# Query pair products from shifted copies on VectorE, in place of selection matmuls and squares on ScalarE

## The chip, the cores and the metric

The kernel runs on one core of one Trainium2 chip. The metric is the device time of one execution in microseconds (us). A profiled execution also has a *span*, from the first to the last instruction; it is about 2 us shorter than the time of the same run. A run is slow here when it took over 1.5% longer than the fastest of the same kernel. Medians and ranges are those of all runs.

A ratio below is the mean time of one kernel's fast runs over the mean of the other's fast runs of the same rounds, with a 95% interval. It is therefore not quite the ratio of the medians that stand beside it.

## The reference, cut to what matters

Two independent attention problems, A and B, have the same shapes: 2048 tokens, width 640, 32 heads of 20. Inputs are bf16.

```python
def _A_ref(x, wqkv, wo):                       # softmax attention
    ...
    scores = jnp.einsum("bhqd,bhkd->bhqk", q, k) * (Dh ** -0.5)
    p = _softmax(scores, axis=-1)
    o = jnp.einsum("bhqk,bhkd->bhqd", p, v)
    return o.transpose(0, 2, 1, 3).reshape(B, S, D) @ wo
def _B_ref(x, wqkv, wo):                       # linear attention
    phi = lambda t: jnp.where(t > 0, t + 1, jnp.exp(t)) + 1e-6
    pq, pk = phi(q), phi(k)
    kv = jnp.einsum("bhsd,bhse->bhde", pk, v);  z = jnp.einsum("bhsd->bhd", pk)
    num = jnp.einsum("bhqd,bhde->bhqe", pq, kv)
    den = jnp.einsum("bhqd,bhd->bhq", pq, z)[..., None] + 1e-6
    o = num / den
    return o.transpose(0, 2, 1, 3).reshape(B, S, D) @ wo
return jnp.concatenate([a, b], axis=-1)
```

Both kernels avoid A's 2048 x 2048 scores. They replace the exponential by a polynomial of second degree. The keys enter through moments (sums over keys of 1, of k, and of products of two components of k, each with the value row), and each query then needs only its own 20 components and its 210 pair products.

## The kernel before

The work has three stages: A's key moments, A's query blocks, and the outputs. B's work is filler. A planner written in Python places every instruction beforehand, so each engine runs a fixed list in order and waits on semaphores. `PB, BK = 3.0, 1.02` are ranks in that planner; a lower number goes first.

A's queries are loaded four heads at a time. Selection matmuls of contraction 32, one for each head, form q_a + q_(a+d) for 110 and then for 100 of the 210 pairs of a head, and ScalarE squares them out of PSUM:

```python
    def t_sel(self, n, k, deps):
        ...
            for i in range(4):
                b = t.bank[i // 2] + i % 2
                sch.mm(ps[0:nb, b, :], self.S2[32 * i:32 * i + 32, 110 * k:110 * k + nb],
                       self.Qr[32 * i:32 * i + 32, s, g, :], start=True, stop=True, ...)
        ...
            def sq(x, p=p):
                b = j.bank[p]
                sch.op("act", lambda e: e.activation(self.psi[0:nb, sp, k, 2 * p:2 * p + 2, :], ps[0:nb, b:b + 2, :],
                                                     AF.Square, scale=sc), ...)
```

The moments are multiplied with q (four matmuls) and with the squares (eight), and VectorE evicts the 20 numerators and the denominator:

```python
    def t_pv(self, n, deps):
        ...
            for i in range(4):
                sch.mm(ps[32 * i:32 * i + 32, b, :], self.Mst[:, g, 32 * i:32 * i + 32], self.Qr[:, s, g, :], ...)
            for k in range(2):
                for i in range(4):
                    sch.mm(ps[32 * i:32 * i + 32, b, :], self.Tu[0:_NB[k], k, g, 32 * i:32 * i + 32],
                           self.psi[0:_NB[k], sp, k, i, :], start=False, stop=(k == 1), ...)
        ...
        def ev(_):
            sch.op("dve", lambda e: e.tensor_scalar(self.OTr[:, pr, u, :], ps[:, j.bank, :], self.cst[:, g:g + 1], 0.0,
                                                    op0=ALU.add, op1=ALU.max, accum_out=self.mx[:, n:n + 1]), ...)
```

Normalisation sends denominators to DRAM, takes reciprocals, reads them back broadcast, multiplies, stores to DRAM (`f_Od`) and reloads the result for the output projection. B's reciprocals also return by broadcast loads, 52 DMAs on SyncE's queue in all.

## Time and profile before

| what | before |
|---|---|
| time, median (range) | 398.18 us (397.9 to 400.53), 3 runs |
| span of the profiled run | 394.6 us |
| TensorE, VectorE, ScalarE busy | 315.4, 251.6, 232.9 us |
| mean granted TensorE clock | 0.905 of full |
| bytes moved by DMA | 42.48 MB |

The first fence is the top of the page of the kernel before. Each digit is the busy share of one fortieth of the span, in tenths; PEclk is the granted clock in tenths.

```profile
span 394.6 us, 14071 instructions
## 1 busy us (share of the span) xinstructions
PE 315.4 (80%) x6356; PEld 179.0 (45%) x6356; DVE 251.6 (64%) x444; ACT 232.9 (59%) x373; POOL 14.2 (4%) x43
## 2 busy tenths in 40 slices
PE   4278997999999899598879787787896896357485
PEld 1256766877676577432222233232342443235142
DVE  5859985876846988966625264575664877354431
ACT  1147864564757687448999975769785895010001
POOL 7600000000000000000000000000000000000000
PEclk9999999999999999779966867989898999587789
```

TensorE is near full in the first stage. In the middle ScalarE comes to 9 while VectorE falls and the clock drops. At the end nobody is full. The same by stage (a row is a stretch of time; busy us of each engine, then clock, DMA share and GB/s):

```profile
core 0: us, PE busy (x) PEld busy (x) DVE busy (x) ACT busy (x) POOL busy (x), PEclk, DMA share, GB/s
22.00:141.00 119.00, 112.97 (x3276) 84.17 (x3280) 87.46 (x135) 77.06 (x172) 0.00 (x0) 1.00 0.37 83
141.00:300.00 159.00, 131.73 (x1872) 57.64 (x1864) 98.75 (x176) 123.09 (x160) 0.00 (x0) 0.85 0.29 86
300.00:390.00 90.00, 64.22 (x1194) 33.86 (x1186) 49.16 (x96) 29.06 (x36) 0.00 (x0) 0.85 0.44 142
```

The groups of instructions that the change removes (busy us, mean ns of one, then the idle time before them and what ended it):

```profile
L1457 ACT ACTIVATE f_big<-ps 100x1024 bf16<-100x1024 f32 (+1 forms) x128 | 120.8, 1043 | 16.5 <-PE ps L172 16.3
...
L172 PE MATMUL ps<-f_Qr,f_S 32*110 32x512 bf16 (+1 forms) x256 | 41.4, 472 | 7.5 <-ACT f_big L1457 7.4
...
L1488 DVE TENSOR_SCALAR_CACHE_REDUCE f_xT<-ps,f_c 128x512 f32<-128x512 f32 x32 | 23.6, 736 | 20.1 <-PE ps L172 19.9
```

ScalarE's 120.8 us of squares look like the middle stage's limit: it is the engine with the most work there. That is read from the profile. The selection matmuls that feed them are TensorE time with no attention in it.

### The profile page before, as it was taken

To read this page: it belongs to the slowest core of one execution; us is meant where nothing else is said; L and a number is where in the kernel's file an instruction comes from. 1 tells how busy PE (TensorE), PEld (TensorE's weight loads), DVE (VectorE), ACT (ScalarE), POOL (GpSimd) and SP (SyncE) were. 2 spreads that over 40 slices of the span, in tenths; PEclk is the share of its full clock that TensorE was granted. 3 is DMA by queue.
4 is the path that set the end of the run, shared out by engine and by line. 5 is a ranking of instruction groups with operands and counts; after the bars stand their busy time and mean duration, and the time that the engine had idled before them with its cause. 6 is when DMAs were issued, how large, how long until landed. Compare 5 with 4: busy or idle time off the path is not lost.

```text
span 394.6 us, 14071 instructions
## 1 busy us (share of the span) xinstructions
PE 315.4 (80%) x6356; PEld 179.0 (45%) x6356; DVE 251.6 (64%) x444; ACT 232.9 (59%) x373; POOL 14.2 (4%) x43
## 2 busy tenths in 40 slices
PE   4278997999999899598879787787896896357485
PEld 1256766877676577432222233232342443235142
DVE  5859985876846988966625264575664877354431
ACT  1147864564757687448999975769785895010001
POOL 7600000000000000000000000000000000000000
PEclk9999999999999999779966867989898999587789
DMA  8996580000415201000023434347344644365232
GB/s 291 267 184 90 96 231 30 5 3 5 109 44 156 68 18 43 28 2 8 10 63 107 127 115 130 136 125 173 136 142 127 188 151 130 120 181 184 91 120 71
DMA packets 48913, 42.48 MB, mean 108 GB/s; under 512 B 23024, under 2 KB 44368, under 8 KB 48848
## 3 DMA queue, kind: packets, MB, share of 16 engines
q1 hardware_dynamic: 47536, 39.90, 36.1%
q10 hardware_dynamic: 1312, 1.64, 1.1%
q8 instruction: 50, 0.82, 0.9%
q14 instruction: 15, 0.12, 0.1%
HBM read 26.26 MB, written 10.83 MB: 94 GB/s over the span
## 4 chain that ended last, share of the span: by engine, by line
PE 43%; DMA 24%; DVE 17%; ACT 7%; issue 3%; SPq 3%; POOL 2%; DVEq 0%; POOLq 0%; ACTq 0%
PE ps L172 43%; DMA f_Rbc<-f_Nd 11%; DMA out_dram<-f_st 5%; DVE f_big L1298 4%; DMA f_big<-f_Nd 3%; ACT f_big L1457 3%; DMA f_w<-f_Od 3%; DVE f_r L1620 2%; DMA f_Nd<-f_Rc 2%; ACT f_ex L1624 2%; DVE f_big L1303 2%; DVE f_CT L1182 2%; SPq L1552 1%; DVE f_st L1069 1%; DVE f_OTw L1543 1%
## 5 line engine op out<-in xcount | busy, mean ns | idle before, releaser
L1457 ACT ACTIVATE f_big<-ps 100x1024 bf16<-100x1024 f32 (+1 forms) x128 | 120.8, 1043 | 16.5 <-PE ps L172 16.3
L172 PE MATMUL ps<-f_w,f_xT 128*32 128x320 bf16 x1280 | 49.7, 307 | 3.7 <-DVE f_xT L1069 3.7
L1069 DVE CAST f_st<-ps 128x320 bf16<-128x320 f32 x57 | 27.3, 486 | 35.3 <-PE ps L172 27.4
L172 PE MATMUL ps<-f_Qr,f_S 32*110 32x512 bf16 (+1 forms) x256 | 41.4, 472 | 7.5 <-ACT f_big L1457 7.4
L172 PE MATMUL ps<-f_wB,f_xB 128*32 128x320 bf16 x1280 | 45.9, 299 | 1.0 <-ACT f_ex L1624 1.0
L172 PE MATMUL ps<-f_woB,f_pk 128*32 128x320 bf16 x640 | 31.9, 356 | 14.7 <-DVE f_pk L1807 7.3
L1620 DVE TENSOR_SCALAR f_r<-ps 128x320 f32<-128x320 f32 (+1 forms) x52 | 29.2, 565 | 19.5 <-PE ps L172 12.1
L172 PEld LDWEIGHTS ps<-f_w,f_xT 128*32 128x32 bf16 x1280 | 34.6, 99 | 14.5 <-DVE f_xT L1069 4.0
L172 PEld LDWEIGHTS ps<-f_wB,f_xB 128*32 128x32 bf16 x1280 | 34.0, 97 | 11.9 <-ACT f_ex L1624 1.6
L1624 ACT ACTIVATE f_ex<-ps 128x320 f32<-128x320 f32 (+1 forms) x52 | 25.3, 498 | 22.9 <-DVE f_r L1620 14.5
L172 PE MATMUL ps<-f_wo,f_w 128*32 128x320 bf16 (+1 forms) x584 | 28.7, 325 | 10.4 <-DMA f_w<-f_Od 8.9
L1488 DVE TENSOR_SCALAR_CACHE_REDUCE f_xT<-ps,f_c 128x512 f32<-128x512 f32 x32 | 23.6, 736 | 20.1 <-PE ps L172 19.9
L1065 ACT CAST f_st<-ps 128x320 bf16<-128x320 f32 x7 | 2.9, 427 | 56.3 <-PE ps L172 34.8
L172 PEld LDWEIGHTS ps<-f_woB,f_pk 128*32 128x32 bf16 x640 | 18.6, 113 | 27.5 <-DVE f_pk L1807 8.5
L172 PE MATMUL ps<-f_xB,f_wB 128*32 128x512 bf16 x400 | 29.5, 426 | 1.9 <-ACT f_ex L1624 1.8
L172 PEld LDWEIGHTS ps<-f_Qr,f_S 32*110 32x110 bf16 (+1 forms) x256 | 12.3, 127 | 41.1 <-ACT f_big L1457 20.6
L1298 DVE TENSOR_TENSOR f_big<-f_big,f_Ks 128x3200 bf16<-128x3200 bf16 x16 | 28.9, 1820 | 1.8 <-ACT f_Ks L1065 1.8
L172 PE MATMUL ps<-f_big,f_Tu 110*32 110x512 bf16 (+1 forms) x256 | 26.2, 441 | 1.1 <-ACT f_big L1457 0.9
L172 PEld LDWEIGHTS ps<-f_wo,f_w 128*32 128x32 bf16 (+1 forms) x584 | 16.3, 103 | 22.3 <-DMA f_w<-f_Od 10.0
L1065 ACT CAST f_big<-ps 128x320 bf16<-128x320 f32 x29 | 12.1, 427 | 23.6 <-PE ps L172 21.9
L172 PE MATMUL ps<-f_xT,f_w 128*32 128x512 bf16 x400 | 23.8, 379 | 1.1 <-ACT f_Vp L1065 1.1
L1303 DVE TENSOR_TENSOR f_big<-f_big 128x2560 bf16<-128x2560 bf16 x16 | 23.7, 1484 | 0.0
(114 smaller groups left out, 369.0 us busy)
## 6 DMA issues: line engine op xcount, KB each, us to landing
out_dram<-f_st SPq DMA_DIRECT2D x32, 160.0 KB
f_Rbc<-f_Nd SPq DMA_DIRECT2D x8, 512.0 KB
f_big<-f_Nd SPq DMA_DIRECT2D x7, 512.0 KB
f_w<-f_Bd SPq DMA_DIRECT2D x12, 240.0 KB
f_Qd<-f_qkp SPq DMA_DIRECT2D x20, 128.0 KB
f_Qr<-f_Qd SPq DMA_DIRECT2D x16, 160.0 KB
f_wB<-in_B_wqkv_dram SPq DMA_DIRECT2D x3, 800.0 KB
f_Od<-f_OTw SPq DMA_DIRECT2D x60, 40.0 KB
```

Source lines behind the costliest of these rows:

```text
L172: lambda e: e.matmul(out, lhsT, rhs, start=start, stop=stop, tile_position=tp, skip_group_check=sgc),
L1065: return self.sch.op("act", lambda e: e.copy(out, in_), reads=reads, writes=writes)
L1069: return self.sch.op("dve", lambda e: e.tensor_copy(out, in_), reads=reads, writes=writes)
L1182: sch.op("dve", lambda e: e.tensor_copy(self.CT0[:], self.ident[:, 0:110]), reads=("ident",), writes=("CT0",))
L1298: sch.op("dve", lambda e: e.tensor_tensor(F[:, :, 112:212].rearrange("p h (d a) -> p h d a", a=20), k0.unsqueeze(2).broadcast_to([128, 32, ...
L1303: sch.op("dve", lambda e: e.tensor_tensor(F[:, :, 22:102].rearrange("p h (d a) -> p h d a", a=20), k0.unsqueeze(2).broadcast_to([128, 32, ...
L1457: sch.op("act", lambda e: e.activation(self.psi[0:nb, sp, k, 2 * p:2 * p + 2, :], ps[0:nb, b:b + 2, :], AF.Square, scale=sc), reads=(("ps" ...
L1488: sch.op("dve", lambda e: e.tensor_scalar(self.OTr[:, pr, u, :], ps[:, j.bank, :], self.cst[:, g:g + 1], 0.0, op0=ALU.add, op1=ALU.max, ac ...
L1543: sch.op("dve", lambda e: e.tensor_tensor(self.OTw[:, ow], self.OTr[:, pr], self.Rbc[rb], op=ALU.mult), reads=(("Rbc", rb, 0), ("Rbc", rb, ...
L1552: self.ost[P] = self.spd([lambda e, i=i: e.dma_start(dst(i), self.OTw[32 * i + 1:32 * i + 21, ow, :, :]) for i in range(4)], (m,), (("OTw" ...
L1620: sch.op("dve", lambda e: e.tensor_scalar(r1, ps[:, j.bank, 0:n], 0.0, 1e-6, op0=ALU.max, op1=ALU.add), reads=(("ps", j.bank),), writes=(( ...
L1624: sch.op("act", lambda e: e.activation(ex, ps[:, j.bank, 0:n], AF.Exp), reads=(("ps", j.bank),), writes=(("ex", k, h),))
```

## The change

Intent: six heads a block, so that 6 x 20 = 120 partitions are filled, and the pair products made as bf16 products on VectorE, q_a times q_(a+d), with the shift made by reading the queries from DRAM at another row. A full block loads six copies into a slot of 12 planes of 512 queries, VectorE makes ten planes of products out of them in three instructions (the last three over copies that are no longer wanted), ScalarE squares one plane, and TensorE multiplies all 12 with masked moments. There are 24 blocks (per 512 queries five of six heads, one of two heads) and three slots, so a slot is loaded again as soon as its block is multiplied.

```diff
-    NQR = 4
-    NPS = 3
+    NS = 3
+    NO = 9
+    NQK = 6
...
+    def t_psi(self, n, deps):
+        s = n % self.NS
+        sl = self.slot[0:120, s]
+        if c < 5:
+            fns = [lambda e: e.dma_start(sl[:, 0:4, :], self.q_load(c, qc, 0, 4, 1, True)),
+                   lambda e: e.dma_start(sl[:, 9:11, :], self.q_load(c, qc, 7, 2, 3, True))]
+        else:
...                                            # short block: six small loads
+            if c < 5:
+                mul(4, 9, 0, 4, (k0, k1, k2), (("sl", s, "A"),))     # 4 planes, 2048 elements
+                mul(8, 10, 0, 3, (k0, k1, k2), (("sl", s, "B"), k1)) # 3 planes
+                mul(1, 0, 1, 3, (k0, k2), (("sl", s, "C"), k2))      # 3 planes
...
     def t_pv(self, n, deps):
+            xs = (0, 1, 2, 3, 4, 5, 6, 7, 8, 9, 10, 11) if c < 5 else (1, 2, 3, 4)
+            for x in xs:
+                lhs = self.Tu[0:m, x, c, :] if c < 5 else self.TuS[0:m, x - 1, :]
+                self.fm(ps[0:126, b, :], lhs, self.slot[0:m, s, x, :], start=(x == xs[0]), stop=(x == xs[-1]), ...)
...                                            # normalisation in groups of three blocks,
...                                            # 25 small constants on GpSimd, masks for the moments
-        PB, BK = 3.0, 1.02
+        PB, BK = _C["bq"], _C["bk"]           # 4.77 and 2.57
```

The order changes too: A's keys now outrank B's keys and values, whose rank goes from 1.02 to 2.57. B's queries rank last of all, at 4.77.

## The prediction

> **What bounds it now (394.6 us profiled, 398.2 median).** Busy time by stretch shows three stages.
> - 22 to 164 us: key moments of A, with B's keys and values as filler. TensorE is busy 132.9 of 142 us at clock 1.00.
> - 172 to 335 us: A's queries. ScalarE is busy 130.7 of 163 us, 120.8 of it squares. TensorE shows 134.8, but in short bursts: by the waits it waits 33 us for squares; the granted clock is 0.87. Selection matmuls (41.4 us by group) stream only about 14 us of columns.
> - 335 to 395 us: the last outputs. TensorE works 34.7 of 60 us; the chain of waits runs through a 12.9 us broadcast, a 7.3 us reload, an 8.5 us store.
>
> **Removed.** ScalarE: 126 us of squares. TensorE: selection 41.4, linear term 15.5, moment matmuls 32.7: 90 us as the profile counts. VectorE: evictions with a maximum 26, normalisation 26, a 6.5 us start-up copy beside a 7 us GpSimd memset.
>
> **Added.** VectorE products: 2048+1536+1536 elements for 20 blocks, 2048 for four. Like products now do 3200 elements in 1.82 us, 2560 in 1.48, so 3.0 us and 1.3 us: 65 us. The Trainium skill ("VectorE: DVE Perf Modes", "What auto-detection actually checks") says an all-16-bit two-source product takes the two-results mode; 1.75 elements per ns agrees. Normalisation in threes 21 us, masks on the moments 12, guard 3. VectorE goes from 252 to an estimated 270, some copies moving to ScalarE, which falls from 233 to about 155.
> TensorE: 256 passes of 512 columns at the 0.24 us of today's dense query projection (23.8 us/100): 61 us, plus guard 7, building moments 5 to 8, projection 2. TensorE lands near 300 against 315, but denser.
> DMA: about 17 MB of shifted query loads and 2.6 MB of stores, minus 5: 42 to about 57 MB; DMA share in the query stage from 0.38 to perhaps 0.6; loads take 5 to 8 us, which three slots should cover.
>
> **Critical path.** A's moments now outrank B's keys and values, so they end after about 22 + 16 x 4.5 (VectorE features per tile) = 100 to 115 us instead of 164, plus some 12 us for masked moments. B's dense projections then fill TensorE beside the query blocks. The squares' bottleneck and most bubbles of 172 to 335 go; B's queries and reciprocals are made early, so part of the tail's 25 us of idle TensorE goes. A floor: 20 start + 295 TensorE work + 8 last store = 323. VectorE at 270 of some 330 us is the second limit, and the two will not interleave perfectly: add about 30.
>
> **Predicted: 352 us**, 8 in 10 within 332 to 382. Faster by over 2%: 0.88; within 2%: 0.06; slower by over 2%: 0.06.
>
> **Right if the profile shows:** products near 1.2 and 0.9 us; VectorE busy 255 to 285, ScalarE 140 to 170, TensorE 285 to 315; first query block between 110 and 140 us; mean clock above the present 0.905 (the skill's "TensorE: Matmul & The Clock Gate", "What's actually happening", ties a half clock to idle windows; the low clocks of 172 to 335 sit where TensorE works in bursts); TensorE busy over 85% of the span.
>
> **Wrong if:** products miss the fast mode (+60 us of VectorE, no gain); query loads queue behind broadcasts so that blocks wait over 8 us for their slot; the last A block's five DMAs (9 to 12 us each now) are uncovered, a 40 us tail; small GpSimd constant copies delay the first K tile past 25 us; or denser matmuls bring the clock down.

## The result

| what | before | after |
|---|---|---|
| time, median (range), 4 runs each | 398.04 us (396.21 to 400.53) | 380.5 us (377.5 to 380.68) |
| ratio | | 0.9546, 95% interval 0.9482 to 0.961 |
| span | 394.6 us | 375.7 us |
| TensorE, VectorE, ScalarE busy | 315.4, 251.6, 232.9 us | 307.5, 261.6, 166.5 us |
| mean clock | 0.905 | 0.927 |
| DMA | 42.48 MB | 58.02 MB |

The change is faster by 4.5%, some 18 us, where 46 were forecast. The page of the kernel after:

```profile
span 375.7 us, 14905 instructions
## 1 busy us (share of the span) xinstructions
PE 307.5 (82%) x6814; PEld 204.6 (54%) x6814; DVE 261.6 (70%) x371; ACT 166.5 (44%) x353; POOL 11.7 (3%) x43
## 2 busy tenths in 40 slices
PE   5079899999998999897899888869867995647485
PEld 3056677887665569766577444423434562534354
DVE  6149999899979871786987998976968685330200
ACT  2049788897761462435254434322313421034043
POOL 2600000000011000000000000000000000000000
PEclk9569999999997999999999999986996999899769
```

The same stretches of time, after:

```profile
core 0: us, PE busy (x) PEld busy (x) DVE busy (x) ACT busy (x) POOL busy (x), PEclk, DMA share, GB/s
22.00:141.00 119.00, 113.92 (x2875) 81.44 (x2871) 106.08 (x123) 85.23 (x182) 2.78 (x3) 0.96 0.45 106
141.00:300.00 159.00, 137.77 (x2878) 86.58 (x2874) 124.08 (x174) 58.19 (x118) 0.00 (x0) 0.95 0.60 176
300.00:390.00 90.00, 49.40 (x1038) 33.05 (x1026) 22.09 (x33) 19.85 (x48) 0.00 (x0) 0.92 0.40 130
```

In the middle ScalarE falls from 123 to 58 us and VectorE rises from 99 to 124, as the change intends. TensorE's idle time there goes from 27.3 us (159 less 131.7) to 21.2, and no further. After 300 us it works 49.4 of 75.7 us, so 26.3 us are idle. From 22 us on it works 301.1 us (the sum of the three rows) and idles 52.6.

The groups that took the place of the old ones:

```profile
L1572 DVE TENSOR_TENSOR f_big<-f_big 120x1536 bf16<-120x1536 bf16 (+2 forms) x68 | 67.6, 1002 | 7.0 <-DMA f_big<-f_Qd 5.6
L172 PE MATMUL ps<-f_big,f_Tu 120*32 120x512 bf16 (+2 forms) x960 | 59.1, 381 | 4.8 <-DVE f_big L1572 3.3
```

The products of 2048 elements took 1.217 us and those of 1536 took 0.957 us. The Trainium skill's page "VectorE: DVE Perf Modes" ("Side-by-side: where the cycles go for N=2048 bf16") gives 1224 ns for 2048 elements in the mode with two results a cycle; this trace agrees.

The loads of the copies, in the list of DMA issues (KB each, median us from issue to landing), beside the output stores. These medians stand on few transfers: the trace records the landing of three of each twenty loads (4.8 to 5.1 us and 7.1 to 7.8 us) and of two of the 32 stores (9.3 us in the query stage, 1.8 us for the last store of the run).

```profile
f_big<-f_Qd SPq DMA_DIRECT2D x20, 480.0 KB, 5.1
out_dram<-f_st SPq DMA_DIRECT2D x32, 160.0 KB, 5.5
...
f_big<-f_Qd SPq DMA_DIRECT2D x20, 240.0 KB, 7.3
```

The waits of the whole run that look large at first sight (total us, times, longest):

```profile
ACT f_st L1079 <- DMA out_dram<-f_st: 49.7, 8, 14.6
...
PEld ps L172 <- ACT f_st L1079: 18.2, 10, 6.5
```

Following every block through the trace gives the cycle of one slot. These are means over blocks 3 to 23, in us, decoded from the start and end of the instructions; they are not a view of the profile. "Free to" is the time from the slot's release to the next load's issue. "Landing and queue" runs from the end of the last load's issue to the first product, and so holds the landing and the wait for VectorE's turn.

```
                     free to   issuing  landing   products  wait for  matmuls | last block
                     load               and queue           matmuls           | ends at
after                 0.94      2.29     11.41      2.84      0.80      2.75  |  299.2
```

A slot is held about 21 us, and the blocks end one per 6.7 us (from the end of the first to the end of the last). That the one sets the other is not shown; e_prod below speaks against it. The longest waits of TensorE's matmuls between 141 and 300 us, of 21.2 us idle there, are for products of the ring (f_big), for nothing that the profile shows ("issue"), and for output staging (f_st):

```profile
PE ps L172 <- DVE f_big L1572: 6.6, 7, 2.8
PE ps L172 <- issue: 6.4, 6, 2.1
PE ps L172 <- ACT f_st L1079: 6.0, 1, 6.0
```

### The profile page after: what moved, and what is told of

The parts are those of the page before. It is cut to its first block, busy times and chain, and to the rows that moved or that the text cites. A ratio compares the mean times of both kernels' runs of the same rounds, so it can differ in the third digit from the quotient of the medians.

```text
span 375.7 us, 14905 instructions
## 1 busy us (share of the span) xinstructions
PE 307.5 (82%) x6814; PEld 204.6 (54%) x6814; DVE 261.6 (70%) x371; ACT 166.5 (44%) x353; POOL 11.7 (3%) x43
## 2 busy tenths in 40 slices
DMA packets 62414, 58.02 MB, mean 154 GB/s; under 512 B 20520, under 2 KB 58824, under 8 KB 62344
## 4 chain that ended last, share of the span: by engine, by line
PE 51%; DMA 17%; DVE 13%; SPq 7%; issue 4%; ACT 4%; POOL 2%; POOLq 0%; DVEq 0%; ACTq 0%
PE ps L172 51%; DMA out_dram<-f_st 9%; DMA f_big<-f_Qd 7%; SPq L1892 3%; SPq L1559 3%; DVE f_big L1572 2%; DMA f_w<-f_Od 2%; DVE f_big L1331 1%; DVE f_big L1326 1%; DVE f_r L1717 1%; DVE f_Tu L1429 1%; ACT f_ex L1721 1%; POOL f_P L1213 1%; ACT f_st L1079 1%; DVE f_pk L1731 1%
## 5 line engine op out<-in xcount | busy, mean ns | idle before, releaser
L1572 DVE TENSOR_TENSOR f_big<-f_big 120x1536 bf16<-120x1536 bf16 (+2 forms) x68 | 67.6, 1002 | 7.0 <-DMA f_big<-f_Qd 5.6
L172 PE MATMUL ps<-f_big,f_Tu 120*32 120x512 bf16 (+2 forms) x960 | 59.1, 381 | 4.8 <-DVE f_big L1572 3.3
L1079 ACT CAST f_st<-ps 128x320 bf16<-128x320 f32 x64 | 25.9, 430 | 65.1 <-DMA out_dram<-f_st 49.7
L172 PEld LDWEIGHTS ps<-f_big,f_Tu 120*32 120x32 bf16 (+1 forms) x960 | 31.8, 96 | 26.5 <-DVE f_big L1572 6.4
L1079 ACT COPY f_xT<-ps 126x512 f32<-126x512 f32 (+1 forms) x29 | 16.9, 586 | 58.4 <-PE ps L172 52.3
L172 PE MATMUL ps<-f_wo,f_w 128*32 128x320 bf16 x640 | 29.6, 319 | 10.0 <-DMA f_w<-f_Od 4.7
L1331 DVE TENSOR_TENSOR f_big<-f_big 128x3200 bf16<-128x3200 bf16 x16 | 29.0, 1814 | 0.0
L172 PEld LDWEIGHTS ps<-f_wo,f_w 128*32 128x32 bf16 x640 | 19.5, 102 | 17.4 <-DMA f_w<-f_Od 8.8
L172 PE MATMUL ps<-f_xT,f_w 128*32 128x512 bf16 (+2 forms) x440 | 28.5, 403 | 0.5 <-issue 0.5
L1079 ACT COPY f_Ks<-f_big 128x608 bf16<-128x608 bf16 (+1 forms) x32 | 19.1, 596 | 1.0
```

Of the source, the lines that this page charges most:

```text
L172: lambda e: e.matmul(out, lhsT, rhs, start=start, stop=stop, tile_position=tp, skip_group_check=sgc),
L1079: return self.sch.op("act", lambda e: e.copy(out, in_), reads=reads, writes=writes)
L1331: sch.op("dve", lambda e: e.tensor_tensor(F[:, :, 22:122].rearrange("p h (d a) -> p h d a", a=20), k0.unsqueeze(2).broadcast_to([128, 32, ...
L1572: return e.tensor_tensor(x[:, o:o + n, :], x[:, a:a + 1, :].broadcast_to([p, n, 512]), x[:, b:b + n, :], op=ALU.mult)
```

## The experiments

Theories when the experiments began. **D**: the traffic of the shifted copies costs time, because it slows every DMA round trip, above all the slot's own. **R**: the output stores wait for two staging tiles. **I**: the time to issue DMAs on SyncE's single queue. **V**: VectorE, with 262 us of work, is the new limit. **S**: the start is late. Later came **T**, A's last chain of DMAs, and **B**, B's late denominators. Each kernel was timed in three rounds against the kernel before on the same chip; the kernel before had medians of 394.5 to 396.4 us in these batches. The kernel after, run again in the second batch, had a median of 381.78 us (378.65 to 382.21), ratio 0.9656 [0.9572, 0.9741]:

> The changed kernel itself again, as the reference of this batch: 377 to 382 us by every theory.

### Staging tiles: e_ring, e_actq, e_ring_actq

The largest wait in the list, 49.7 us of ScalarE for output stores, is the obvious suspect. e_ring gives each problem four staging tiles in dead memory. e_actq issues the 32 output stores from ScalarE's queue and not from SyncE's. The third does both.

```diff
-            s = t % 2                                   # e_ring
+            s = (0, 1, 6, 7)[t % 4]
-                sg = 2 + t % 2
+                sg = 2 + t % 4
-            self.stg[s] = self.spd([lambda e, t=t, s=s: # e_actq
+            self.stg[s] = self.actd([lambda e, t=t, s=s:
```

> The changed kernel with four output tiles in staging for each of the two problems instead of two (the extra ones lie in memory that is free by then). Theory R, the two-tile ring: ScalarE's 49.7 us of waits for stores and TensorE's 14 to 18 us of waits for the casts behind them go, and the time falls by 8 to 14 us. Theory Q, the in-order SyncE queue is what holds the tail: under 3 us. Theory V, VectorE's 262 us set the pace, and theory D, DMA traffic: within 2 us.

> The changed kernel with the 32 output stores issued from ScalarE's queue, right behind its own casts, instead of SyncE's; staging stays at two tiles. Theory Q: SyncE's 30 us of waits for casts go, the last block of B gets its reciprocals and broadcasts some 10 us sooner, and the time falls by 6 to 14 us. Theory R: under 3 us, since a tile still waits for its store to land. Theories V and D: within 2 us.

> Both edits. If R and Q are separate costs, the sum, 14 to 24 us; if they are one wait seen twice, no more than the larger of the two alone. Under V or D: within 3 us.

Measured: 380.63 us, ratio 0.9666 [0.9551, 0.9781]; 378.26 us (one run slow; 377.22 by the fast ones), 0.9602 [0.9499, 0.9705]; 380.02 us, 0.9614 [0.9523, 0.9705]. In e_ring this wait fell from 49.7 to 14.1 us and no time came back: other waits (for B's broadcasts, for the reload of A's result) took its place. R falls for the kernel as it stands. The longest wait in the list was ScalarE's; TensorE's weight loads waited 18.2 us in its wake, and even so its removal alone was worth nothing.

### The start: e_start

In the kernel after, VectorE builds B's block mask behind 25 small constant copies on GpSimd, and A's first transposes to SBUF stand behind that mask in VectorE's list. The start of the kernel after, in the waits from 0 to 25 us:

```profile
PE ps L172 <- DVE f_xT L1083: 11.7, 1, 11.7
DVE f_r L1237 <- POOL f_Rbc L1234: 9.5, 5, 7.8
```

e_start moves the mask ahead of the copies. It computes the same.

```diff
         self.mid_consts()
+        self.p_consts()          # the 25 copies, now after the masks
```

> The changed kernel with B's mask constants made before the 25 small GpSimd copies of the selection constants, so that VectorE is not held for 7.8 us at the start and the first key tile starts near 13 us instead of 21. Theory S, every microsecond of TensorE's start counts because it is busy to 300 us: 5 to 8 us less. If the end is set by the tail's own waits or by VectorE: under 3 us.

Measured: 374.25 us (373.15 to 376.1), ratio 0.9474 [0.9376, 0.9572]. By medians that is 6 us less than the kernel after; by ratios 3 to 7, with overlapping intervals. The profile says where: the first row of e_start below against the same stretch of the kernel after, where TensorE had 6.44 us of work in it. The first query block's matmuls come at 134.5 us and not 141.8. (The ratios' intervals overlap, so how much of the 6 us is real is not settled; all four runs of e_start are faster than all runs of the kernel after.)

```profile
0.00:22.00 22.00, 14.29 (x216) 8.75 (x220) 13.71 (x46) 8.32 (x17) 10.96 (x37) 0.77 1.03 257
```

### Issue time: e_bact

SyncE spends 228 us of the run issuing DMAs (200 before, summed over the trace). e_bact moves the 52 broadcasts of B's reciprocals to ScalarE's queue.

```diff
-                m3 = self.spd(fns, (m2, rbprev[k], bar), ...)
+                m3 = self.engd("act", fns, (m2, rbprev[k], bar), ...)
```

> The changed kernel with the 52 small broadcasts of B's reciprocals issued from ScalarE's queue instead of SyncE's. They cost SyncE about 0.7 us each, 35 us in all, and in the trace 8 to 13 of them stand in front of the last normalisation store and the last reload of A. Theory I, issue time on one in-order queue holds the tail: 8 to 15 us less. If ring, VectorE or DMA traffic holds it: within 3 us.

Measured: 383.93 us (382.03 to 387.69), ratio 0.9748 [0.9649, 0.9847]. No gain, although this took SyncE's issuing from 228 to 190 us. I, for these issues, falls.

### VectorE or traffic: e_prod, e_load, e_lp, e_lp_dummy

e_prod makes one plane per product and not four, three and three; TensorE reads the same amount. e_load fetches two copies in place of six. Both compute wrong pair products. The comparison with the reference is too coarse to see the second-order part. e_lp is both.

```diff
-                mul(4, 9, 0, 4, ...)                                        # e_prod: likewise B and C
+                mul(4, 9, 0, 1, ...)
-            fns = [... e.dma_start(sl[:, 0:4, :], self.q_load(c, qc, 0, 4, 1, True)),   # e_load
-                   ... e.dma_start(sl[:, 9:11, :], self.q_load(c, qc, 7, 2, 3, True))]
+            fns = [... e.dma_start(sl[:, 0:1, :], self.q_load(c, qc, 0, 1, 1, True)),
+                   ... e.dma_start(sl[:, 9:10, :], self.q_load(c, qc, 7, 1, 3, True))]
```

> Wrong result on purpose: each of the three products of a full query block makes one row set instead of 4, 3 and 3, so about 1.1 us of VectorE a block instead of 3.1 (40 us less in all); TensorE runs the same number of matmuls. Theory V, VectorE limits: 10 to 25 us less. Theories of the tail, or TensorE: under 4 us.

> Wrong result on purpose: a full query block loads two shifted copies instead of six, 240 KB instead of 720 KB, so 9.6 MB of 58 MB of traffic go and the number of DMAs stays. Theory D, DMA traffic stretches loads, broadcasts and stores: 6 to 15 us less, and the landing time of output stores below 4 us from 5.5. Otherwise: within 3 us.

e_prod: 380.61 us (379.25 to 384.91), ratio 0.9688, with VectorE's busy time down from 261.6 to 226.0 us. Nothing: V falls for the kernel as it stands. Its last block ends at 299.6 us, like the kernel after's. The trace shows what took the place: products took 1.5 us less a block, the blocks then waited 2.2 us and not 0.8 for their matmuls, and a slot was held 21.0 us as before. TensorE waited 2.9 us for products and not 6.6 in the query stage, but 11.2 for output staging and not 6.0. Short products together with four staging tiles were not run.

e_load: 367.06 us (365.97 to 370.81), ratio 0.933 [0.9238, 0.9421]; 14.7 us less than the kernel after in the same batch, with 9.83 MB fewer moved. Its DMA issues:

```profile
f_big<-f_Qd SPq DMA_DIRECT2D x56, 120.0 KB, 3.5
out_dram<-f_st SPq DMA_DIRECT2D x32, 160.0 KB, 4.7
```

The output stores' 4.7 us against 5.5 is again a median of two landings: the one recorded in the query stage took 7.5 us and not 9.3, the last of the run 1.8 us in both. (Below 4 us was expected.) The stretch of the query blocks now has a DMA share of 0.42 where the kernel after had 0.60, and TensorE works 5.2 us more in it:

```profile
141.00:300.00 159.00, 142.95 (x3033) 82.59 (x3027) 134.28 (x195) 61.35 (x125) 0.00 (x0) 0.99 0.42 134
```

The last block ends at 285.0 us against 299.2, one block per 6.16 us and not 6.72. TensorE's longest waits from 141 to 286 us, to be set beside those of the kernel after:

```profile
PE ps L172 <- DVE f_big L1572: 7.5, 9, 1.9
PE ps L172 <- DVE f_mx L1609: 2.3, 2, 1.4
PE ps L172 <- ACT f_st L1079: 2.2, 1, 2.2
```

The wait for the ring's products did not fall (7.5 us, before 6.6), and "landing and queue" is 11.1 us a block and not 11.4. What fell is the rest: the unexplained waits (6.4 us) are gone and the staging wait is 2.2 us. Up to its last block TensorE idles 12.7 us (21.2 in the kernel after), and its busy time from 141 us on is 131.3 us and not 137.0, at a clock of 0.99 and not 0.95. So the bytes were worth 14.7 us, but not by a shorter wait for the slots.

e_load changes two things, what a block waits for and how many bytes move. (It also cuts SyncE's issuing from 228 to 211 us; e_bact cut it further and gained nothing.) e_lp_dummy takes e_lp and adds one load of 360 KB per full block into planes that nobody reads in that kernel.

```diff
+            if c < 5:
+                sch.dma("sp", lambda e: e.dma_start(sl[:, 5:8, :], self.q_load(c, qc, 1, 3, 1, True)),
+                        reads=(("Qd", c, qc),), writes=(("dum", s),))
```

> Wrong result on purpose: the two-copy load and the short products together, as the base for the next run. Products alone did nothing, so 364 to 370 us as with the two-copy load alone, by either theory.

> Wrong result on purpose: as the run before, but behind each small load a further 360 KB goes from DRAM into rows of the slot that nobody reads, and nobody waits for it but the next such transfer of the slot. It puts back three quarters of the traffic that was taken out, without its wait. Theory D, traffic volume: back up by 6 to 12 us. Theory L, the landing time of the load that a block waits for: under 4 us more.

e_lp: 362.67 us (361.76 to 368.85; one run slow, 362.29 by the fast ones), ratio 0.913 [0.9083, 0.9177]. With the loads cut, shorter products are worth something, which they are not in e_prod. e_lp_dummy: 373.17 us (372.17 to 375.67), ratio 0.9427 [0.9373, 0.9481]: 10.5 us (10.9 by fast runs) come back with 7.4 MB that no block waits for. The first half of D stands: it is the traffic that costs, and not only a block's own longer load. (The added loads also cost SyncE 15 us of issuing, and a fixed order shifted with them, so the 10.5 us are not traffic to the last bit.) How it costs is not shown. All these loads go through SyncE's queue, so bytes that fill the DMA engines and bytes that stand in front of other transfers in that queue were never told apart; the copies on another queue were not run.

### A fourth slot: e_ns4

Four slots in place of three, paid for by cutting the ring of evicted blocks from nine to six.

```diff
-    NS = 3
-    NO = 9
+    NS = 4
+    NO = 6
```

> The changed kernel with a fourth query slot, in memory that is dead by then (the ring of evicted blocks shrinks from 9 to 6 for it); same traffic. Theory L, the slot ring: a slot is held 21 us in the trace (issue 2.3, landing and VectorE's turn 11.4, products 2.8, matmuls 2.8 and small waits), a third of that is the 6.7 us between blocks; with four slots TensorE's waits on loads and products between 141 and 300 us shrink, and the time falls by 5 to 14 us. Theory D, traffic volume: within 3 us of the changed kernel.

Measured: 398.04 us, ratio 1.0025 [0.9981, 1.007]. The blocks' products were ready and then waited 9.5 us on average for their matmuls, which by code and trace is a wait for the normalisation of the blocks evicted before them. That hides what a fourth slot is worth, so the question stays open. It suggests that nine evicted blocks are not a luxury.

### The order alone: b_order

The kernel before with B's keys and values ranked 2.57, as in the kernel after.

```diff
-        PB, BK = 3.0, 1.02
+        PB, BK = 3.0, 2.57
```

> The kernel before with one number changed: the priority of B's keys and values falls from 1.02 to 2.57, as in the change, so that A's moments come first; selection matmuls and squares stay. If the order alone is worth what the change gained: 376 to 386 us. If the products are needed for it, since ScalarE must still do 126 us of squares beside B's exponentials: 390 us or more.

Measured: 396.79 us, ratio 1.0033 [0.9961, 1.0104]. This part of the new order alone is worth nothing (B's queries kept their rank of 3.0): the gain needs the rest of the change.

### Do the terms add, and what holds the tail: e_tail, e_start_load, e_start_load_tail

The tail is the time after the last query block, from 299 to 376 us. e_tail lets the last normalisation group take the reciprocals of an earlier group, already in DRAM, so that its read, its reciprocal and its store fall away. Its output is wrong, which doesn't matter for the time.

```diff
-        d1 = self.spd([...Rc...], evs, ...)
+        d1 = None if G == 7 else self.spd([...Rc...], evs, ...)   # likewise the reciprocal and its store
```

> The last normalisation group of A takes the reciprocals of an earlier group, already in DRAM, so its read of the denominators, its reciprocal and its store fall away and its broadcast can land before the last block ends (wrong result on purpose: three of 24 blocks get the wrong divisor). Tail theory T (A's last chain of DMAs sets the end): the last multiplication comes at about 305 instead of 336 us, TensorE's idle time after 300 us falls from 26.6 us to about 10, and the time falls by 10 to 20 us, to 360 to 370 us. Rival F (B's own broadcasts and output stores fill the end anyway, the SyncE queue paces it): 0 to 4 us less.

> The start of e_start (mask constants first) together with the two-copy loads of e_load (wrong result on purpose). e_start alone gave about 6 us, e_load alone 14.7 us. If both causes are separate pieces of the missing gain: 357 to 363 us, ratio to before about 0.915. If the start's gain is swallowed because the query stage then waits for the same traffic: 366 or more.

> All three taken away: late start, copies' traffic, last normalisation round trip (wrong result on purpose). If the three are the missing gain, this lands at the predicted 352 us or under, 342 to 353. If the tail is filled by B anyway, it stays within 3 us of the run without the tail change, 356 to 362.

e_tail: 376.99 us (376.18 to 380.15), ratio 0.9565 [0.9488, 0.9641]. It lies within the kernel after's 0.9546 to 0.9656, so no gain is shown, and T falls: in its trace A's last store of results was only ten us earlier (330.0 for 340.3), and TensorE idled as long after 300 us (25.2 us).

e_start_load: 360.93 us (359.57 to 362.36), ratio 0.912 [0.9057, 0.9183]. Start and traffic are separate terms and add: 6 and 14.7 us alone, 20 together.

e_start_load_tail: 356.16 us (353.42 to 360.45; one run slow, 355.75 by the fast ones), ratio 0.9047 [0.8965, 0.9129]; some 5 us less than without the tail change, but the intervals overlap. It is the closest any run came to the predicted 352 us.

### B's queries first: e_bq, e_start_actq_bq

In the kernel after, the last denominators of B are read at 319.4 us, no earlier than before (one line each, of the kernel before, then of the kernel after; first and last start are the two times at the end):

```profile
L1760 SPq DMA_DIRECT2D f_dc<-f_dn x4: 632/644/720, 185.0 to 317.4; - x4
```

```profile
L1865 SPq DMA_DIRECT2D f_dc<-f_dn x4: 642/858/1530, 235.2 to 319.4; - x4
```

e_bq ranks B's query projections before its keys and values.

```diff
-..., bq=4.77, ...
+..., bq=2.3, ...
```

> One number of the static order: B's query projections rank before B's keys and values instead of last of all (4.77 to 2.3), so B's last query projection stands before A's last block in TensorE's order, and not after it. That is what the prediction took for granted when it said that B's queries and reciprocals are made early; in the kernel after, the last denominators go to DRAM at 319 us, 20 us after the last block. Theory B (late denominators of B and the broadcasts that wait for them hold the tail): last denominators by about 300 us, TensorE idle after 300 us falls from 26.6 to under 18, time 368 to 374. Rival S (in order on one SyncE queue, with stores waiting for two staging tiles, the tail takes as long whichever comes first): 377 to 383, no gain.

Measured: 402.55 us median, two of four runs slow. The two fast ones took 397.94 and 399.3 us, 18 us more than the kernel after; no ratio is given for so few. The two theories expected less time or the same, and both were wrong in sign. The trace shows how. The last denominators do come earlier, but the first come later, and all broadcasts that follow them move to the end (e_bq; then the broadcasts of the kernel after):

```profile
L1865 SPq DMA_DIRECT2D f_dc<-f_dn x4: 613/627/642, 247.8 to 303.0; - x4
...
L1892 SPq DMA_DIRECT2D f_wB<-f_Bd x52: 514/730/3466, 295.6 to 363.3; - x52
```

```profile
L1892 SPq DMA_DIRECT2D f_wB<-f_Bd x52: 521/718/2003, 256.1 to 349.8; - x52
```

B's keys and values are hardly later (the masking of their sums begins at 224.6 us and not 223.4). But the first denominators come 12.6 us later, and in SyncE's list the first broadcast, at 295.6 us, now stands behind the loads of A's last block (issued from 287.3 us). 47 of 52 broadcasts start after 300 us (29 in the kernel after), and A's last reload starts at 362.0 us and not 350.6, behind those broadcasts. Why the planner placed them so was not followed further.

### A correct kernel that beats both: e_start_actq

e_start and e_actq together; nothing is computed wrongly.

> A correct kernel: the mask constants first, and the 32 output stores issued from ScalarE's queue. Alone they gave 6 us and 0 to 3 us. Expected 371 to 375 us, ratio to before 0.935 to 0.95; not distinguishable from the start alone (374) if the stores' gain was noise.

Measured: 367.39 us (366.61 to 367.82), ratio 0.9299 [0.9238, 0.936], against 395.16 us of the kernel before. That beats both the kernel before and the kernel after, and is better than the sum of its parts. Its last block ends at 286.6 us (292.6 in e_start), and 20 of the 52 broadcasts remain after 300 us. Why the stores' queue is worth 7 us with the early start and little without it was not tested. The Trainium skill's page "DMA: Bandwidth & Descriptors" ("Rules for kernel authors") says that spreading DMAs over issuing engines brings no bandwidth and only saves time to issue; e_actq and e_bact, with no clear gain, agree, and these 7 us do not contradict it, since they may be issue time.

The same with B's queries first:

> A correct kernel: e_start_actq with B's query projections before its keys and values. If the tail was held by late denominators: 357 to 364 us. If not, within 3 us of the 367.4 of e_start_actq. If the order that suits one start is bad for another: slower than 370.

Measured: 376.73 us (375.73 to 379.9), ratio 0.9562 [0.9471, 0.9653]; 9 us slower, as e_bq would have it.

## Why the prediction was right and wrong

**Right as far as tested: what limits the kernel before.** The squares went, ScalarE fell by 66 us and the time fell. B's keys and values in the new order alone gave nothing (b_order). Selection matmuls and squares went together, so their shares in the gain are not told apart.

**Right: what each engine costs.** VectorE 261.6 us (forecast 255 to 285), ScalarE 166.5 (140 to 170), TensorE 307.5 (285 to 315), products 1.217 and 0.957 us (near 1.2 and 0.9), 58.02 MB (about 57), DMA share 0.60 in the query stage (perhaps 0.6), mean clock 0.927 (above 0.905). The first query block's matmuls began at 141.8 us, just outside 110 to 140. TensorE was busy for 82% of the span, not over 85%. The clock is right partly by luck: the prediction tied it to the end of the bursts that the squares cause, but b_order, with all its squares, had 0.918 to 0.936 in its four runs and was no faster.

**Wrong: the idle time of TensorE.** The forecast sum was 20 start + 295 TensorE work + 8 last store + "about 30" = 353. The measured span of 375.7 is 22 before the first stage's work + 301.1 work + 52.6 idle. Work is 6 us over and idle time about 15 us over its 38 (8 and 30). Of the idle time 5.1 us lie between 22 and 141 us, 21.2 in the query stage and 26.3 after 300 us. The median run, 380.5 us, lies another 5 above that span, 2 of them because a time is longer than its span.

**The step that failed** is "loads take 5 to 8 us, which three slots should cover". It was a statement about cost: covered loads cost nothing, so the traffic that the prediction had counted to within about 1 MB was given no price. The loads did land about as said (4.8 to 7.8 us, six recorded). But taking 9.83 MB away gave 14.7 us back (e_load), and returning 7.4 MB that nobody waits for cost 10.5 (e_lp_dummy). By which path is open. The slot ring is the nearest suspect: a slot is held not for a load alone but through issuing, landing, VectorE's turn, products and matmuls, about 21 us. Yet shorter products left those 21 us as they were (e_prod), and without the bytes TensorE waited for the ring's products as long as before (7.5 and 6.6 us); what went were its other waits and the lower clock. The Trainium skill's page "DMA: Bandwidth & Descriptors" ("Latency and other measured facts") says that the fixed part of a DMA grows with the load on the memory; the one store recorded in the query stage, at 9.3 and 7.5 us, agrees in direction, but from its issue on it may also have stood behind other transfers, so no run here shows the fixed part alone.

**A second step** is the start. "Small GpSimd constant copies delay the first K tile past 25 us" was listed as a danger. It came in at 21.1 us, so the danger by its own measure did not arise, yet the copies held VectorE for 7.8 us and cost some 6 us by medians (3 to 7 by ratios, e_start).

**A third** is "B's queries and reciprocals are made early, so part of the tail's 25 us of idle TensorE goes". They were not: the last denominators are read at 319.4 us (317.4 before), and the tail has 26.3 us idle. The rank of 4.77 stood in the diff and was read as an order among B's parts only. The step would not have helped by itself either: making B's queries early costs 18 us (e_bq).

**The sum.** With start and traffic taken away the kernel runs at 360.9 us, and with the last normalisation shortened too at 356.2, so these account for about 24 of the 28 us between 380.5 and 352. The third part is not shown by itself.

**Open.** What a fourth slot is worth without a smaller ring of evicted blocks. What holds the tail's idle 26 us: four staging tiles, another queue for the broadcasts, A's last round trip and the rank of B's queries were each tried on the kernel after, and none shortened the run beyond the spread. And how the 14.7 us of traffic come about: by the slots' round trip, by other DMAs that queue behind the copies on SyncE's queue, or by busy DMA engines.

## What to carry to other kernels

When work moves from an engine to the memory system, price the bytes and not only the engine's time: here each MB of extra loads cost about 1.5 us (14.7 us for 9.83 MB), with the DMA engines busy for 0.60 of the query stage. Charge a ring of buffers for the whole time that a buffer is held, and check that slots times period covers it; but test that the ring is the limit before lengthening it, since here, with each engine's list in a fixed order, the waits that e_ring and e_prod took away were replaced by others. And distrust the longest wait in a list: 49.7 us were worth nothing, while a 7.8 us wait at the start, and a load share that no wait list names, were worth the most.

## What the Trainium skill lacked or had wrong

- "DMA: Bandwidth & Descriptors" gives an access latency of the memory for an average and a high load, but no landing time of a whole transfer by what else moves. Here the one store of 160 KB that was recorded in the query stage landed in 9.3 us where the DMA share was 0.60, and in 7.5 us where it was 0.42; the last store of each run landed in 1.8 us.
- The same page names the time to issue a DMA and gives no figure for a whole issue on SyncE. Here broadcasts took 0.72 us each (median), and 228 us of a 376 us run went into issuing.
